# First phase of an attention-and-MLP kernel: the first two hidden pieces' products split by rows of x and put between the units, one score bank instead of two, more idle transposes, another order

## Chip, cores and metric

One core of one Trainium2 chip. The metric is device time in microseconds of one execution. Three runs of the kernel before took 499.43, 497.88 and 498.04 us (median 498.04).

## What is computed

```python
f = 1 / (1 + exp(-f_logit))                        # (4, 8, 768, 48): batch, head, time, dim
for t in range(768):
    state = f[t][:, None] * state + outer(k[t], v[t])
    y[t] = q[t] @ state
x = y.transpose(0, 2, 1, 3).reshape(3072, 384)     # 8 heads of 48
out = relu(x @ w_in) ** 2 @ w_out                  # w_in 384 x 2048, w_out 2048 x 384
```

## The kernel before

**Tiling.** Time is cut into 6 blocks of 128 steps; a block has 512 tokens (4 batches of 128). A block's attention is done in 4 units: units 0 to 2 of a block hold two heads' 48 rows on partitions 0 to 47 and 64 to 111 and, in the 16 rows behind each, a slice of two more heads; unit 3 of a block works on those slices, which DMAs gather into `last_kq`, and has no gates, keys and queries of its own. Units are numbered through: 0 to 3 are block 0, 4 to 7 block 1. In tile names `ds1_0` is block 1, unit 0 of it, that is unit 4.

**The MLP.** The hidden layer is cut into 16 pieces of 128. `up` multiplies a piece of w_in with the block's x: x has three tiles of 128 rows, and each product is three matmuls of fp32r halves (low by high, high by low, high by high), so nine matmuls of 128x512 into one bank `ph`. `square` (ACT, three passes) and `rest` (DVE) make the halves of relu squared, `down` adds nine matmuls into three banks `po`. The weights come as fp32 words in 64-bit form and are decoded on the chip by ACT and DVE (`bits`, `parts`), 12 of the 32 halves before the main passes, in five steps each.

**The first phase.** Blocks 0 and 1 of the attention, the decoding of six pieces and these pieces' products with block 0 stand in two lists of steps, `FIRST` and `SECOND`, executed by `step`; they set by hand the order on TensorE (PE), VectorE (DVE), ScalarE (ACT) and the DMA queue of SyncE (SP). GpSimd (POOL) is ordered by a scheduler. Behind `SECOND`, `flow` runs the main passes: nothing but products, with the later blocks' attention hooked in.

A step is a letter and a number, of the unit or of the piece:

- L, f, k, v load a unit's data, i and o a piece's halves of w_in and w_out (SP). G is the sigmoid (ACT). K and Q are keys and queries: a scan and a product each on DVE, and the reciprocal of Q waits for POOL.
- T transposes the keys (PE), N copies them out (ACT). S and D are the score and state matmuls (PE) into one pair of banks `ds`; M masks the scores and C updates the states (DVE).
- r and s bring rows of queries and states across the partitions: ACT copies in block 0, DMAs in block 1. m gathers a unit's slices into `last_kq`.
- Y gives the outputs (PE), H casts them to the high half of x (ACT); z takes that off on PE in block 0, and X writes the low half (ACT in block 0, DVE in block 1). g and h move unit 3's rows into x by DMA.
- A I V c J are the five steps of decoding a half of w_in (ACT, DVE, DVE, ACT, DVE), B O Z d P of w_out, e n t a w of the rows of w_in that unit 3's tile is multiplied with (`w4`).
- u is a piece's `up` with x0, x1 and x2, U of pieces 0 and 1 the three matmuls with unit 3's tile, U of later pieces the whole `up`. R is `square`, E is `rest`, W is `down`.
- busyN is N transposes of the identity that nobody reads.

In PSUM the first list has one bank `ps_h0` for `ph`, one for the key transposes, a pair that `first_py` and then all of block 1's `ds` and `py` share, and two pairs (`ps_p`, `bufs=2`) for `ds` of units 0 to 3. `ps_h1` and the three `ps_o` are opened behind `FIRST` in the place of `ps_p`. The idle transposes write into the bank of piece 0. `finish_last` copies out the last block: tile 2 in two halves by ACT and DVE, both into one tile `ob`.

Of the kernel before, what the change touches and what calls it, by code (L numbers as in the profile page):

```python
# [13 lines left out]
F32 = mybir.dt.float32  # L14
# [10 lines left out]
P = 128  # L25
# [7 lines left out]
NT = B * TB  # L33
# [3 lines left out]
NJ = DM // P  # L37
# [41 lines left out]


class Moe:
# [268 lines left out]
    def finish_last(self, c, dst):  # L350


        nc, half = self.nc, NT // 2
        self.cur = c
        for e in range(NJ):
            self.down(c.fs[-1], (e,))
        for e in range(NJ):
            ob = self.const.tile([P, NT], F32, tag=f"w{2 + e}_0", name=f"ob{c.blk}_{e}")
            if e < NJ - 1:
                (nc.vector.tensor_copy if e % 2 else nc.scalar.copy)(out=ob, in_=c.po[e])  # L360
                nc.sync.dma_start(dst(e), ob)
                continue
            nc.scalar.copy(out=ob[:, :half], in_=c.po[e][:, :half])  # L363
            nc.vector.tensor_copy(out=ob[:, half:], in_=c.po[e][:, half:])  # L364
            nc.sync.dma_start(dst(e)[:, :half], ob[:, :half])
            nc.sync.dma_start(dst(e)[:, half:], ob[:, half:])
# [10 lines left out]
def fast_path(ctx, psum, tc, moe, ident, low, flag, fkqT, vN, w, w4, out):  # L377
    nc = tc.nc
# [310 lines left out]
    half = list(range(LO)), list(range(LO, NF))  # L689
# [8 lines left out]
    def unit(n):  # L698
        if n not in units:
            units[n] = Unit(n, xs, (ps_a, ps_p) if n < HP else (ps_a,))  # L700
        return units[n]

    def step(t):

        nm = t.rstrip("0123456789")
        n = int(t[len(nm) :])
        if nm == "busy":
            if 0 not in moe.cur.ph:
                moe.bank(0)
            for _ in range(n):
                nc.tensor.transpose(out=moe.cur.ph[0][:, 0:P], in_=ident, identity=ident)
        elif nm in ("i", "o"):
            weights_load(n, "io".index(nm))  # L720
# [249 lines left out]
@with_exitstack  # L970
def tile_kernel(ctx: ExitStack, tc: tile.TileContext, fkqT, vN, w, w4, out):
    nc = tc.nc
    const = ctx.enter_context(tc.tile_pool(name="const", bufs=1))
    ident = const.tile([P, P], F32, name="ident")
    low = const.tile([P, NBLK * NJ, B * NC], F32, name="low")
    sums = const.tile([P, 2 * NF], F32, name="sums")
    flag = const.tile([1, 1], I32, name="flag")
    moe = Moe(ctx, tc, const, sums, out)
    with ExitStack() as fast:
        last, rv = fast_path(fast, ctx, tc, moe, ident, low, flag, fkqT, vN, w, w4, out)  # L980

# [6 lines left out]
    last.g[NF - 1] = moe.held  # L990
    moe.finish_last(last, lambda e: out[last.blk, e * P : (e + 1) * P])
# [61 lines left out]
```

## Time and profile before

| what | value |
|---|---|
| median of 3 runs | 498.04 us |
| profiled execution, its own time | 498.81 us |
| its span, first to last instruction | 497.1 us |
| mean granted clock of TensorE | 0.979 |
| busy: PE, DVE, ACT | 96%, 52%, 56% of the span |
| end of the step W5, first matmul of the main passes | 75.15 us |
| last matmul's end | 492.43 us |

The busy shares are means over a first phase of 75 us and a uniform rest of 417 us. The first phase has to be read by itself: by stretches, with PE's granted clock in each, and then in order of time. 1.7 us of the profiled time lie around the span.

### The profile page before, as it was taken

What the parts mean: (1) busy time and instruction counts of PE and PEld (TensorE: products, weight loads), DVE (VectorE), ACT (ScalarE), POOL (GpSimd) and SP (SyncE); (2) the same over time, 40 slices, a digit from 0 to 9 for tenths busy, and PEclk for the clock granted to TensorE, in tenths of its full rate; (3) what the DMA queues carried; (4) which work ended last, traced back from release to release, by engine and by line L of the source; (5) the groups of instructions that cost most, each with busy time, mean ns of one, the idle gap of its engine ahead of it and who ended that gap; (6) DMA issues with size and microseconds to landing.
All of it is one profiled execution on the core that took longest, in us unless ns stands there. A gap on an engine that the chain in (4) does not pass through costs nothing. (4 is left out here: it accounts for less than half of the span.)

```text
span 497.1 us, 11384 instructions
## 1 busy us (share of the span) xinstructions
PE 478.9 (96%) x4778; PEld 390.4 (79%) x4778; DVE 257.4 (52%) x472; ACT 280.2 (56%) x568; POOL 29.1 (6%) x66
## 2 busy tenths in 40 slices
PE   5879999999999999999999999999999999999995
PEld 4757786888888878888888888888888888888884
DVE  6998877999865363645353446254255331122111
ACT  4776667887847464555455554555546454544441
POOL 6221010001000000000000000000000000000000
PEclk8689999999999999999999999999999999999999
DMA  8876327473312204413005413004320001100001
GB/s 287 256 235 199 85 46 272 136 255 126 91 30 80 75 7 117 144 28 91 3 1 123 143 29 92 1 1 116 100 78 13 3 0 33 63 2 3 0 0 69
DMA packets 22684, 42.68 MB, mean 86 GB/s; under 512 B 4464, under 2 KB 8176, under 8 KB 22624
## 3 DMA queue, kind: packets, MB, share of 16 engines
q1 hardware_dynamic: 22176, 40.94, 27.0%
q0 software_dynamic: 448, 0.92, 0.8%
q8 instruction: 39, 0.64, 0.5%
q14 instruction: 21, 0.17, 0.1%
HBM read 31.69 MB, written 4.72 MB: 73 GB/s over the span
## 5 line engine op out<-in xcount | busy, mean ns | idle before, releaser
L251 PE MATMUL ph<-x,w 128*128 128x512 f32 x864 | 217.6, 397 | 1.2 <-DVE gl L268 1.2
L251 PEld LDWEIGHTS ph<-x,w 128*128 128x128 f32 x864 | 160.1, 189 | 35.8 <-DVE gl L268 2.0
L278 PE MATMUL po<-gh,w 128*128 128x512 f32 x570 | 175.6, 389 | 0.0
L268 DVE TENSOR_TENSOR gl<-ph,gh 128x512 fp32r<-128x512 f32 x95 | 65.6, 690 | 187.7 <-ACT gh L263 183.2
L261 ACT ACTIVATE ph<-ph 128x512 f32<-128x512 f32 x96 | 55.9, 582 | 144.9 <-PE ph L251 144.9
L278 PEld LDWEIGHTS po<-gh,w 128*128 128x128 f32 x570 | 107.1, 188 | 22.2
L278 PE MATMUL po<-gl,w 128*128 128x512 f32 x285 | 111.2, 390 | 0.0
L278 PEld LDWEIGHTS po<-gl,w 128*128 128x128 f32 x285 | 53.5, 188 | 11.2
L262 ACT ACTIVATE ph<-ph 128x512 f32<-128x512 f32 x96 | 55.9, 582 | 3.0
L263 ACT CAST gh<-ph 128x512 fp32r<-128x512 f32 x95 | 55.8, 587 | 3.0
L467 POOL TENSOR_SCALAR fkq<-fkq 128x8 f32<-128x8 f32 x18 | 11.9, 663 | 306.3 <-DVE fkq L462 305.8
L176 ACT CAST w<-wa 128x384 fp32r<-128x384 f32 (+1 forms) x33 | 16.6, 512 | 14.1 <-DVE wa L163 10.3
L462 DVE TENSOR_TENSOR_SCAN fkq<-fz,dr 128x520 f32<-128x520 f32 x18 | 22.2, 1235 | 4.0 <-ACT fz L457 4.0
L603 PEld LDWEIGHTS py<-sc,vn 64*64 64x64 f32 (+1 forms) x640 | 18.1, 126 | 7.1 <-issue 7.1
L476 DVE TENSOR_TENSOR_SCAN fkq<-fz,dz 128x520 f32<-128x520 f32 x18 | 22.4, 1242 | 0.6
L565 DVE TENSOR_TENSOR sc<-ds,mask 128x512 f32<-128x512 f32 x24 | 16.6, 690 | 11.1 <-PE ds L558 9.3
L603 PE MATMUL py<-sc,vn 64*64 64x64 f32 (+1 forms) x640 | 21.4, 222 | 0.0
L615 PE MATMUL py<-rx,sx 48*48 48x64 f32 (+1 forms) x320 | 20.4, 217 | 0.1
L142 ACT ACTIVATE wa<-raw 128x384 f32<-128x384 f32 (+1 forms) x33 | 18.1, 551 | 2.7 <-DMA raw<-in_w_dram 2.7
L159 DVE SCALAR_TENSOR_TENSOR wa<-raw,wa 128x384 int32<-128x384 int32 (+1 forms) x33 | 18.0, 552 | 0.7
L628 ACT CAST x<-py 112x512 fp32r<-112x512 f32 x15 | 8.8, 587 | 16.7 <-PE py L615 16.7
L615 PEld LDWEIGHTS py<-rx,sx 48*48 48x48 f32 (+1 forms) x320 | 18.0, 127 | 0.2 <-ACT sx L497 0.2
(105 smaller groups left out, 399.8 us busy)
## 6 DMA issues: line engine op xcount, KB each, us to landing
fkq<-in_fkqT_dram SPq DMA_DIRECT2D x17, 768.0 KB, 5.5
raw<-in_w_dram SPq DMA_DIRECT2D x32, 384.0 KB, 3.7
vn<-in_vN_dram SPq DMA_DIRECT2D x24, 192.0 KB, 4.8
out_dram<-ob SPq DMA_DIRECT2D x14, 256.0 KB, 2.2
x<-ys SPq DMA_DIRECT2D x30, 64.0 KB, 2.4
last_kq<-fkq SPq DMA_DIRECT2D x28, 64.5 KB, 2.4
out_dram<-part SPq DMA_DIRECT2D x3, 256.0 KB, 2.1
last_kq<-fkq POOLq DMA_DIRECT2D x8, 64.5 KB, 4.3
```

Source lines behind the costliest of these rows:

```text
L142: nc.scalar.activation(a, upper_f, AF.Abs, scale=2.0**-112, **kw)
L159: nc.vector.scalar_tensor_tensor(out=h, in0=upper, scalar=-(1 << 31), in1=h, op0=ALU.bitwise_and, op1=ALU.bitwise_or)
L251: self.nc.tensor.matmul(self.cur.ph[f], lhsT=w[:, i], rhs=x[:, j], start=first and n == 0, stop=last and n == 2)
L261: nc.scalar.activation(ph, ph, AF.Relu)
L262: nc.scalar.activation(ph, ph, AF.Square)
L263: nc.scalar.copy(out=gh, in_=ph)
L268: self.nc.vector.tensor_tensor(out=gl, in0=self.cur.ph.pop(f), in1=gh.bitcast(F32), op=ALU.subtract)
L278: self.nc.tensor.matmul(c.po[e], lhsT=l, rhs=r, start=f == c.fs[0] and i == 0, stop=f in c.ends and i == 2, skip_group_check=len(c.ends) > 1,)
L462: V.tensor_tensor_scan(out=rr[:, ::-1], data0=self.fz[:, NZ * CZ : 0 : -1], data1=dr[:, ::-1], initial=0.0, op0=ALU.mult, op1=ALU.add,)
L476: V.tensor_tensor_scan(out=pp, data0=self.fz[:, : NZ * CZ], data1=dz, initial=0.0, op0=ALU.mult, op1=ALU.add)
L603: nc.tensor.matmul(self.py[h * C : h * C + m, c, b * C : (b + 1) * C], lhsT=self.vn[rows, b, h * D : h * D + m], rhs=self.sc[rows, h, b], ...
L615: nc.tensor.matmul(self.py[h * C : h * C + m, c, b * C : (b + 1) * C], lhsT=s[rows, b * D : b * D + m], rhs=q[rows], start=False, stop=b = ...
```

## The change

It does five things.

1. `up` takes the tiles of x to multiply with. Step u becomes three: p is the three matmuls with x0, q those with x1, u those with x2. p0 stands behind X0, q0 and u0 behind X1 and X2, and p1, q1, u1 and U1 ahead of Y4.
2. `ps_h1` is open from the start, so pieces 0 and 1 have a bank each in the first list.
3. `ps_p` has `bufs=1`: units 0 to 3 share one pair of banks for `ds`.
4. The bank that this frees is `idle`, which the idle transposes write. There are 91 of them in place of 19.
5. `finish_last` gives each copy a tile of its own, so the two halves of tile 2 have separate tiles.

And the two lists stand in another order; u1, U1, R0, E0, W0's forerunners, T5, D5, S5, C5 and M5 have moved from the second list into the first.

```diff
-j0 e0 n0 f0 busy11 busy3 G0 busy2 k0 t0 K0 T0 L1 Q0 G1 v0 K1 S0 N0 D0 M0 i0 A0 I0 T1 L2 o2 L4 C0
-Q1 r0 s0 G2 K2 v1 Y0 N1 H0 z0 X0 D1 S1 B2 i3 Q2 T2 busy3 m1 C1 a0 S2 A3 w0 v2 o1 N2 r1 D2 G4 I3 i1
-M1 s1 K4 v3 A1 Y1 D3 H1 C2 s2 z1 X1 r2 m0 m2 S3 r3 o0 B0 V0 M2 L5 L6 v5 Y2 H2 Q4 r4 v4 C3 s3 G5 I1
-T4 z2 X2 M3 Y3 c0 N4 K5 G6 Q5 V1 H3 z3 X3 T5 S4 D4 o3 B3 J0 m4 r5 B1 C4 c1 s4 u0 O0 U0 M4 Y4
+j0 e0 n0 t0 f0 G0 k0 busy11 a0 busy5 L1 K0 G1 T0 N0 Q0 r0 o2 v0 K1 i0 A0 B2 busy12 S0 D0 Q1 L2 L4
+M0 I0 busy12 C0 s0 v1 i1 busy8 V0 v3 i4 T1 w0 i3 G2 K2 Q2 busy8 v2 N1 c0 r1 D1 S1 C1 m0 Y0 H0 J0
+M1 T2 N2 z0 busy12 G4 o0 X0 K4 p0 S2 D2 A3 s1 Y1 H1 C2 I3 M2 m1 z1 m2 o3 r3 D3 S3 L5 L6 v5 r2 V3
+X1 s2 Y2 c3 busy7 A1 T4 Q4 I1 C3 H2 z2 X2 G5 V1 v6 M3 K5 Q5 r4 q0 u0 s3 B0 O0 Y3 H3 N4 z3 X3 c1 o1
+busy4 J1 G6 U0 S4 R0 B3 v4 D4 p1 B1 C4 E0 q1 o4 u1 U1 Z0 M4 s4 Y4 K6 H4 X4 d0 i5 i2 T5 P0 N5 O1
+busy8 D5 S5 A2 h3 busy4 r5 C5 Z1 d1 M5
...
-J1 Z0 u1 i5 V3 o5 R0 K6 H4 X4 N5 D5 S5 E0 T6 d0 P0 i2 A2 C5 c3 U1 O1 I2 W0 R1 N6 J3 M5 h3 Z1 d1 s5
-Y5 Q6 H5 X5 V2 c2 E1 g3 U3 P1 A5 v6 o4 S6 D6 M6 i4 J2 r6 C6 m5 I5 R3 E3 A4 W1 V5 O3 I4 c5 J5 U2 R2
...
+R1 W0 J3 g3 T6 I2 Q6 s5 m4 r6 N6 Y5 H5 V2 A5 c2 X5 E1 U3 A4 R3 J2 S6 D6 o5 P1 U2 R2 M6 C6 I5 E3 W1
+V5 c5 I4 s6 Y6 V4 H6 J5 v7 m6 U5 O2 Z2 X6 m5 r7 D7 S7 E2 c4 J4 U4 B4 d2 B5 R4 P2 W2 M7 C7 O5 O3 O4
...
-    def up(self, f, last=True):
+    def up(self, f, js=range(NJ), last=True):
...
-        for j in range(NJ):
+        for j in js:
...
-            ob = self.const.tile([P, NT], F32, tag=f"w{2 + e}_0", name=f"ob{c.blk}_{e}")
...
+            for n in (slice(0, NT),) if e < NJ - 1 else (slice(0, half), slice(half, NT)):
+                ob = self.const.tile([P, n.stop - n.start], F32, tag=f"w{2 + at}_0", name=f"ob{c.blk}_{at}")
+                (nc.vector.tensor_copy if at % 2 else nc.scalar.copy)(out=ob, in_=c.po[e][:, n])
+                nc.sync.dma_start(dst(e)[:, n], ob)
+                at += 1
...
-                nc.tensor.transpose(out=moe.cur.ph[0][:, 0:P], in_=ident, identity=ident)
+                nc.tensor.transpose(out=idle, in_=ident, identity=ident)
...
-        elif nm == "u":
-            moe.up(n, last=False)
+        elif nm in "pqu":
+            moe.up(n, ("pqu".index(nm),), last=False)
...
-    moe.psum(psum, "ps_h0")
+    moe.psum(psum, "ps_h0", "ps_h1")
...
-        with tc.tile_pool(name="ps_p", bufs=2, space=bass.MemoryType.PSUM) as ps_p:
+        with tc.tile_pool(name="ps_p", bufs=1, space=bass.MemoryType.PSUM) as ps_p:
+            idle = ps_p.tile([P, 512], F32, tag="idle", name="idle")[:, :P]
...
-        moe.psum(psum, "ps_h1", "ps_o")
+        moe.psum(psum, "ps_o")
```

How it moves instructions, at three places. The first is PE around the first transposes and scores (pk is a unit's transposed keys, ds its scores and states, py or first_py its outputs). Before, from the end of D0:

```order
L547 MATMUL ds0_0_189<-vn0_0_183,kn0_0_206 64x48
L517 MATMUL pk0_1_233<-ident_58,fkq0_1_177 128x128 x4
L603 MATMUL first_py_125<-sc0_0_225,vn0_0_183 48x64 x4
L615 MATMUL first_py_125<-fkq0_0_146,sp0_73 48x64
L615 MATMUL first_py_125<-rx0_0_249,sx0_75 48x64
```

and with the change:

```order
L545 MATMUL ds0_0_221<-vn0_0_195,kn0_0_185 64x48
L714 MATMUL idle_143<-ident_58 128x128 x20
L515 MATMUL pk0_1_296<-ident_58,fkq0_1_173 128x128 x4
L714 MATMUL idle_143<-ident_58 128x128 x8
L545 MATMUL ds0_1_329<-vn0_1_279,kn0_1_322 64x48
```

Unit 1's scores now stand ahead of unit 0's outputs, and 28 idle transposes stand between the scores of units 0 and 1.

The second is PE around the products of pieces 0 and 1 (ph0_0 and ph0_1). Before, from the end of D4 to Y4:

```order
L547 MATMUL ds1_0_589<-vn1_0_524,kn1_0_567 64x48
L251 MATMUL ph0_0_148<-x0_0_116,w0_0_565 128x512 x3
L251 MATMUL ph0_0_148<-x0_1_117,w0_0_565 128x512 x3
L251 MATMUL ph0_0_148<-x0_2_118,w0_0_565 128x512 x3
L251 MATMUL ph0_0_148<-ys0_3_579,w4_343 128x512 x3
L603 MATMUL py1_0_659<-sc1_0_657,vn1_0_524 64x64
```

With the change the products of piece 0 with x0, x1 and x2, and with unit 3's tile, stand in three pieces, of which these are the last two, and D4 is followed by piece 1:

```order
L515 MATMUL pk1_0_585<-ident_58,fkq1_0_259 128x128 x4
L632 MATMUL first_py_125<-x0_2_118,minus_136 112x256 x2
L252 MATMUL ph0_0_424<-x0_1_117,w0_0_325 128x512 x3
L252 MATMUL ph0_0_424<-x0_2_118,w0_0_325 128x512 x3
L601 MATMUL first_py_125<-sc0_3_604,vn0_3_292 48x64 x4
```

```order
L632 MATMUL first_py_125<-ys0_3_651,minus_136 112x256 x2
L714 MATMUL idle_143<-ident_58 128x128 x4
L252 MATMUL ph0_0_424<-ys0_3_651,w4_166 128x512 x3
L556 MATMUL ds1_0_672<-fkq1_0_259 64x64 x16
L545 MATMUL ds1_0_672<-vn1_0_697,kn1_0_653 64x48
```

```order
L545 MATMUL ds1_0_672<-vn1_0_697,kn1_0_653 64x48
L252 MATMUL ph0_1_715<-x0_0_116,w1_0_659 128x512 x3
L252 MATMUL ph0_1_715<-x0_1_117,w1_0_659 128x512 x3
L252 MATMUL ph0_1_715<-x0_2_118,w1_0_659 128x512 x3
L252 MATMUL ph0_1_715<-ys0_3_651,w4_166 128x512 x3
L601 MATMUL py1_0_743<-sc1_0_739,vn1_0_697 64x64
```

Twelve matmuls of piece 0 have gone from behind S4 and D4 to ahead of them, and the twelve of piece 1, which stood behind Y4 in two parts, are together ahead of it.

The third is DVE from the end of Q5 to M4 (wa and w are weights in decoding, sc the masked scores, gl what `rest` writes). Before:

```order
L479 TENSOR_TENSOR fkq1_1_487<-fkq1_1_487 128x512
L159 SCALAR_TENSOR_TENSOR wa1_0_404<-raw1_0_393,wa1_0_404 128x384
L178 TENSOR_TENSOR w0_0_565<-wa0_0_229,w0_0_565 128x384
L580 TENSOR_TENSOR sp0_73<-state0_79,fkq1_0_242 112x192
L587 TENSOR_TENSOR state0_79<-sp0_73,ds1_0_589 112x192
L580 TENSOR_TENSOR sp0_73<-state0_79,fkq1_0_242 112x192
L587 TENSOR_TENSOR state0_79<-sp0_73,ds1_0_589 112x192
L152 SCALAR_TENSOR_TENSOR wa0_1_481<-wa0_1_481,raw0_1_479 128x384
L565 TENSOR_TENSOR sc1_0_657<-ds1_0_589,mask_69 128x512
```

and with the change:

```order
L477 TENSOR_TENSOR fkq1_1_538<-fkq1_1_538 128x512
L153 SCALAR_TENSOR_TENSOR wa0_1_623<-wa0_1_623,raw0_1_417 128x384
L179 TENSOR_TENSOR w1_0_659<-wa1_0_582,w1_0_659 128x384
L578 TENSOR_TENSOR sp0_73<-state0_79,fkq1_0_259 112x192
L585 TENSOR_TENSOR state0_79<-sp0_73,ds1_0_672 112x192
L578 TENSOR_TENSOR sp0_73<-state0_79,fkq1_0_259 112x192
L585 TENSOR_TENSOR state0_79<-sp0_73,ds1_0_672 112x192
L269 TENSOR_TENSOR gl0_0_690<-ph0_0_424,gh0_0_689 128x512
L160 SCALAR_TENSOR_TENSOR wa0_1_623<-raw0_1_417,wa0_1_623 128x384
L563 TENSOR_TENSOR sc1_0_739<-ds1_0_672,mask_69 128x512
```

Before, V1 and J0 stood between Q5 and C4; they have gone ahead of Q5, O0 and J1 stand in their place, and E0 with Z0 has come between C4 and M4.

## Rows read from the trace of the kernel before

**Rows 1.** From the profile's page: busy time of each engine, and the span in 40 slices of 12.4 us (busy tenths of PE, granted clock of PE in tenths).

```profile
PE 478.9 (96%) x4778; PEld 390.4 (79%) x4778; DVE 257.4 (52%) x472; ACT 280.2 (56%) x568; POOL 29.1 (6%) x66
...
PE   5879999999999999999999999999999999999995
...
PEclk8689999999999999999999999999999999999999
```

**Rows 2.** Busy time of each engine by stretch of the span: from:to, length, busy us and instructions, granted clock of PE, DMA share, GB/s.

```profile
8.50:22.06 13.56, 11.19 (x205) 9.01 (x209) 12.92 (x21) 8.86 (x23) 3.76 (x8) 0.50 0.97 330
22.06:32.32 10.26, 7.22 (x278) 5.92 (x272) 9.76 (x17) 9.12 (x22) 2.02 (x4) 1.00 0.79 241
32.32:39.10 6.78, 6.03 (x79) 5.07 (x77) 5.78 (x13) 4.00 (x10) 1.94 (x5) 0.50 0.58 146
39.10:75.20 36.10, 35.03 (x562) 27.87 (x562) 30.04 (x60) 23.99 (x52) 3.90 (x8) 1.00 0.40 112
75.20:492.50 417.30, 415.68 (x3654) 339.08 (x3652) 193.93 (x352) 230.78 (x456) 11.54 (x24) 1.00 0.22 67
```

**Rows 3.** PE in order of time, from S4 to the first matmul of the main passes: start, duration of the group, engine, line, operation, tiles, count, idle time before it and what ended that. S4, u0, U0, u1, T6, U1, the end of D6, and the first products of the main passes.

```profile
34.69 1.13 PE L558 MATMUL ds<-fkq 48*64 48x64 f32 x32
36.58 3.54 PE L251 MATMUL ph<-x,w 128*128 128x512 f32 x9
39.95 0.86 PE L251 MATMUL ph<-ys,w 112*128 112x512 f32 x3
...
41.84 2.33 PE L251 MATMUL ph<-x,w 128*128 128x512 f32 x9
...
45.19 0.66 PE L517 MATMUL pk<-ident,fkq 128*128 128x128 f32 x4
45.60 0.93 PE L251 MATMUL ph<-ys,w 112*128 112x512 f32 x3
...
54.34 0.37 PE L547 MATMUL ds<-vn,kn 64*64 64x48 f32 x10 [1.04 <-issue]
...
75.15 4.24 PE L251 MATMUL ph<-x,w 128*128 128x512 f32 x18
```

**Rows 4.** The same view of PE earlier: the first idle transposes, T0, and z2 (the matmuls that take off the high half of x2).

```profile
1.59 3.64 PE L718 MATMUL ph<-ident 128*128 128x128 f32 x16 [1.59 <-POOL ident masks.py:199]
8.37 1.07 PE L517 MATMUL pk<-ident,fkq 128*128 128x128 f32 x4 [3.14 <-DVE fkq L468]
...
28.75 0.49 PE L634 MATMUL first_py<-x,minus 112*112 112x256 f32 x2 [0.17 <-ACT x L628]
```

**Rows 5.** DVE in order of time: the end of K1, then without a gap C3, I1 (a decoding step), M3, K5 and Q5 to the step behind it.

```profile
11.62 0.69 DVE L468 TENSOR_TENSOR fkq<-fkq 128x512 f32<-128x512 f32 x1
...
28.75 0.35 DVE L580 TENSOR_TENSOR sp<-ds,last_kq 112x192 f32<-112x192 f32 x1
29.14 0.35 DVE L587 TENSOR_TENSOR state<-sp,ds 112x192 f32<-112x192 f32 x1
29.41 0.55 DVE L152 SCALAR_TENSOR_TENSOR wa<-wa,raw 128x384 int32<-128x384 int32 x1
29.88 0.68 DVE L565 TENSOR_TENSOR sc<-ds,mask 128x512 f32<-128x512 f32 x1
30.48 1.23 DVE L462 TENSOR_TENSOR_SCAN fkq<-fz,dr 128x520 f32<-128x520 f32 x1
31.74 0.69 DVE L468 TENSOR_TENSOR fkq<-fkq 128x512 f32<-128x512 f32 x1
32.56 0.21 DVE L474 RECIPROCAL dz<-fkq 128x8 f32<-128x8 f32 x1
...
34.69 0.55 DVE L159 SCALAR_TENSOR_TENSOR wa<-raw,wa 128x384 int32<-128x384 int32 x1
```

**Rows 6.** ACT in order of time: the first pass of a decoding (step B0), H2, G5, and the two copies of N4.

```profile
27.02 0.57 ACT L142 ACTIVATE wa<-raw 128x384 f32<-128x384 f32 x1
...
28.13 0.57 ACT L628 CAST x<-first_py 112x512 fp32r<-112x512 f32 x1
...
29.56 0.63 ACT L457 ACTIVATE fz<-fkq 128x512 f32<-128x512 f32 x1
...
30.97 0.53 ACT L523 COPY kn<-pk 128x448 f32<-128x448 f32 x1
31.40 0.28 ACT L525 COPY last_kn<-pk 128x128 f32<-128x128 f32 x1
```

**Rows 7.** DMA issues in short stretches, KB each and us from issue to landing: v1, issued at 6.83; v4, issued from 30.97; the second DMA of s6.

```profile
vn<-in_vN_dram SPq DMA_DIRECT2D x1, 192.0 KB, 11.2
...
vn<-in_vN_dram SPq DMA_DIRECT2D x1, 192.0 KB, 3.1
...
sx<-sp SPq DMA_DIRECT2D x1, 39.0 KB, 1.9
```

**Rows 8.** All engines in order of time at the end: the copies of the two halves of output tile 2, and the issues of their DMAs.

```profile
492.50 0.37 ACT L363 COPY ob<-po 128x256 f32<-128x256 f32 x1 [0.80 <-DVE ob L360]
492.91 0.42 DVE L364 COPY ob<-po 128x256 f32<-128x256 f32 x1 [0.40 <-ACT ob L363]
492.97 0.39 SPq L365 DMA_DIRECT2D out_dram<-ob  x1
493.45 0.41 SPq L366 DMA_DIRECT2D out_dram<-ob  x1
```

More of the change, by code (lines that the diff above doesn't have):

```diff
@@ L67 @@
 FIRST = """
-j0 e0 n0 f0 busy11 busy3 G0 busy2 k0 t0 K0 T0 L1 Q0 G1 v0 K1 S0 N0 D0 M0 i0 A0 I0 T1 L2 o2 L4 C0
-Q1 r0 s0 G2 K2 v1 Y0 N1 H0 z0 X0 D1 S1 B2 i3 Q2 T2 busy3 m1 C1 a0 S2 A3 w0 v2 o1 N2 r1 D2 G4 I3 i1
-M1 s1 K4 v3 A1 Y1 D3 H1 C2 s2 z1 X1 r2 m0 m2 S3 r3 o0 B0 V0 M2 L5 L6 v5 Y2 H2 Q4 r4 v4 C3 s3 G5 I1
-T4 z2 X2 M3 Y3 c0 N4 K5 G6 Q5 V1 H3 z3 X3 T5 S4 D4 o3 B3 J0 m4 r5 B1 C4 c1 s4 u0 O0 U0 M4 Y4
+j0 e0 n0 t0 f0 G0 k0 busy11 a0 busy5 L1 K0 G1 T0 N0 Q0 r0 o2 v0 K1 i0 A0 B2 busy12 S0 D0 Q1 L2 L4
[4 more added lines that the diff above has]
+busy8 D5 S5 A2 h3 busy4 r5 C5 Z1 d1 M5
 """
 SECOND = """
-J1 Z0 u1 i5 V3 o5 R0 K6 H4 X4 N5 D5 S5 E0 T6 d0 P0 i2 A2 C5 c3 U1 O1 I2 W0 R1 N6 J3 M5 h3 Z1 d1 s5
-Y5 Q6 H5 X5 V2 c2 E1 g3 U3 P1 A5 v6 o4 S6 D6 M6 i4 J2 r6 C6 m5 I5 R3 E3 A4 W1 V5 O3 I4 c5 J5 U2 R2
-m6 O2 V4 Z2 s6 v7 r7 Y6 H6 c4 X6 E2 J4 U5 d2 D7 S7 P2 U4 M7 C7 Z3 B4 B5 R4 s7 W2 O4 O5 d3 Z4 Z5 d4
-d5 P3 Y7 E4 H7 X7 g7 h7 P4 R5 E5 W3 W4 P5 W5
+R1 W0 J3 g3 T6 I2 Q6 s5 m4 r6 N6 Y5 H5 V2 A5 c2 X5 E1 U3 A4 R3 J2 S6 D6 o5 P1 U2 R2 M6 C6 I5 E3 W1
+V5 c5 I4 s6 Y6 V4 H6 J5 v7 m6 U5 O2 Z2 X6 m5 r7 D7 S7 E2 c4 J4 U4 B4 d2 B5 R4 P2 W2 M7 C7 O5 O3 O4
+Z3 d3 Z4 P3 d4 s7 Y7 P4 Z5 H7 X7 E4 R5 E5 W3 W4 g7 d5 P5 W5 h7
 """
@@ L356, in finish_last @@
             self.down(c.fs[-1], (e,))
+        at = 0
         for e in range(NJ):
-            ob = self.const.tile([P, NT], F32, tag=f"w{2 + e}_0", name=f"ob{c.blk}_{e}")
[L359 to L366, printed above, removed]
+            for n in (slice(0, NT),) if e < NJ - 1 else (slice(0, half), slice(half, NT)):
[3 more added lines that the diff above has]
+                at += 1
 def chunks(t):
@@ L714, in step @@
         if nm == "busy":
-            if 0 not in moe.cur.ph:
-                moe.bank(0)
             for _ in range(n):
-                nc.tensor.transpose(out=moe.cur.ph[0][:, 0:P], in_=ident, identity=ident)
+                nc.tensor.transpose(out=idle, in_=ident, identity=ident)
         elif nm in ("i", "o"):
```

## The prediction, made before the change was run

> **What bounds the kernel now.** I read the page first: PE is busy 96% of the span, and its slices are 9 from the third on [rows 1]. Then the stretches, cut where the granted clock changes: behind 39.10 PE runs at 1.00 and is busy 35.03 of 36.10 us, and behind 75.20 it is busy 415.68 of 417.30 [rows 2]. There PE is the limit at its full clock, and apart from the last output copies nothing in the change touches that part. So the change is worth what it moves the handover, the first matmul of the main passes at 75.15 [rows 3]. Ahead of 39 it is otherwise: from 8.50 to 32.32 DVE is busy 12.92 of 13.56 and 9.76 of 10.26 us, while PE stands at the half clock (0.50) up to 22.06 and again from 32.32 to 39.10 [rows 2]. DVE's chain of scans sets the pace there.
>
> Third, PE in order of time: from S4 at 34.69 to the handover PE has work without a gap, but for 1.04 us in the middle of D6 that wait for nothing the profile shows [rows 3]. So the handover is the start of S4 plus the work behind it. I forecast both.
>
> **The work behind S4.** Before it takes 75.15 - 34.69 = 40.5 us. Of that 4.4 us, up to 39.10, run at half clock, which costs 2.2; the stall costs 1.0. Left are 37.2 us of work at full clock. From there the change takes away: u0, nine matmuls, 2.3 us by u1, and U0, three, 0.8 us by the 0.93 of U1 less its latency; they now stand ahead of S4. It brings T5 behind S4, 0.7 us by T6, and 8 + 4 idle transposes. Sixteen took 3.64 us at the start, 0.23 each [rows 4]; T0 took 1.07 there and T6 takes 0.66 at full clock [rows 3, 4], so I take 0.11 each at full clock, 1.4 together. 37.2 - 3.1 + 0.7 + 1.4 = 36.2 us.
>
> **When S4 starts.** Up to the end of K1 at 12.3 [rows 5] DVE's order is unchanged. The prices of DVE's steps, start to start [rows 5]: C in block 0 0.66, a decoding step 0.47, M 0.60, K 1.9, Q 2.1, with about 0.2 when Q has to wait for POOL. Behind K1 now come Q1 (end 14.6), M0, I0, C0, V0, w0 (17.1), K2, Q2 (21.2), C1, J0, M1, K4 (24.8), C2, I3, M2, V3, Q4 (29.6), I1, C3, V1, M3 (32.3), K5, Q5 (36.8), O0, J1 (37.7), C4.
>
> Does PE deliver in time with one score bank and the idle transposes in its queue? T0 at 8.37, 12 idle ones at half clock to 12.0, S0 and D0 to 14.0 at 1 us each: M0 at 14.6 isn't held. By then PE has worked since 8.37; before it worked from 18.1 to 22.06 and the clock rose [rows 2], so I take the full clock from 14 on. 20 idle ones and T1 end at 16.9, N1 at 17.8, D1 waits for v1, which landed at 6.83 + 11.2 = 18.0 [rows 7]; it is the tenth load from the queue in both orders, with the same bytes ahead. S1 ends at 19.3, ahead of C1 at 21.2. Moving o2 ahead of v0 and L2 makes those about 1 us later, hidden: D0 wants v0 at 13. Y0, T2, z0 and 12 idle ones end at 23.0, X0 at 23.2, p0 at 23.9; S2 and D2 end at 25.1, which holds C2 by 0.3. Y1, z1, D3 and S3 end at 28.4, ahead of C3. ACT holds DVE twice: a decoding is 1.1 us there, H 0.6, G 0.6, N 0.7 [rows 6]; A1 ends at 30.0 and holds I1 by 0.4, G5, behind H2 and X2, ends at 32.6 and holds K5 by 0.3. The SP queue: v4 takes v3's buffer and waits for Y3 at 34.1, with o4 and s4 behind it; it lands 3.1 later [rows 7], 37.2, as D4 wants it. L6 waits for Y1 until 26.2, and K6 needs it at 41.
>
> S4 needs X3. M3 ends at 32.3, s3, behind G5, at 32.85; Y3 takes 1.0 (before: from the end of U0, 40.81, to u1 [rows 3]), to 34.0; then H3, N4, X3 on ACT to 36.0, U0 to 36.75. **S4 starts at 36.75**, 2.1 us later than now, since q0, u0 and more decoding stand ahead of it.
>
> **The sum.** 36.75 + 36.2 = 72.95. D5 waits about 0.3 for N5, behind Y4, H4 and d0; hand-overs take 0.2. Behind Y5 no other engine is late: W4's E4 is nearest, 0.1 ahead. Handover at 73.45: **1.7 us earlier**. The part below 39 at full clock pays 2.2 and the stall 1.0; the later S4 takes 2.1 of it, T5 and idle transposes 2.1, and u0 and U0 ahead of S4 give 3.1.
>
> **The tail.** DVE's half copy waited for ACT's, 492.91 against 492.50 [rows 8]; with tiles of its own it runs beside it. But SP issues the two DMAs one behind the other: the second at 493.45 can't go before the first ends at 493.36. Worth 0.05, at most 0.1. Extra matmuls of u cost nothing: the same nine, into the same bank.
>
> The profiled execution took 498.81, its span 497.1; less 1.75 that is 497.06. The median of the runs is 0.77 below the profiled time, so I predict **496.3**.
>
> **Bounds.** The unknown prices are the moment at which the clock rises, the stall, and the waits between engines in the new order. At best the three holds of DVE (1.0 us) and the wait at D5 vanish and X3 comes 1.0 earlier: 1.3 more, 495.0; idle transposes at nothing would be another 1.4, 493.6. At worst, below, 499.2 and more.
>
> [...] The row shows 1.04 us in the middle of D6 with nothing awaited [rows 3]. [...] 72 more transposes, each with its weight load, shift which instruction stands where.
>
> **Rivals.**
> - *Same: the gain is spent on small waits.* A stall like that of D6 comes again (1.0), or the chain to S4 is late by as much: ACT has A3, s1, H1, r3, r2, X1, s2, c3, A1, H2, X2, G5 in one line, and each late one holds DVE, which has no slack until 32 [rows 2]. For it: ACT's line has no gap of 0.3 in my working. Against it: DVE's steps are as long as before, and E0 and M4 only come at 39. Gain 0.3 to 0.9: 497.1 to 497.7.
> - *Slower: the idle transposes hold PE back because the clock doesn't rise at 14.* Between T0 and D1 stand 40 of them, 9.1 us at half clock and 4.4 at full. At half clock up to 22.06 as before, T1 ends at 19.4, N1 at 20.2, D1 and S1 at 22.2, Y0, T2, z0 and 12 idle ones at 26, S2 and D2 at 28.0: C2, I3, M2, K5 and so S4 are 2.9 later. Handover at 76.3, 1.2 later than now: 499.2. From a rise at about 23.5 on it is slower than now by over 1.5 us; at 26, with Y0, T2, z0 and 12 idle ones at half clock as well, by some 4, 502. For it: the first 16 ran at half clock for 3.64 us. Against it: PE worked as long before the rise at 22.06 as it will have at 14. [...]
> - *More: the chain to S4 is shorter*, by the bound above, 495.0.
> - *The change doesn't do what it says.* p0, q0 and u0 could stand ahead of S4 without PE being idle there, if DVE waits for S2 and D2: that is the 0.3 at C2, already in.
>
> **Chances.** The forecast with the case of more gain, over 0.3% faster (1.5 us, about what a measurement of this kernel can tell from no change): 0.48. The small waits, within 0.3%: 0.34, with the clock rising late but by 23 among it. Slower by over 0.3%: 0.18, nearly all of it the clock or a wait on PE's queue that I don't see. The range of 8 in 10 goes from 494.3, most of the better bound, to 499.6, the slower rival's 499.2 and a little: what is left out is 502 and the case without idle transposes' price. The forecast's own range is 495.0 to 497.0.
>
> **What would show it.** Right: S4 near 36.7 with PE's clock at 1.00 from about 14 and no fall to 0.50 behind it; p0 near 23.5; C1 without an idle row ahead of it; PE's rows without a gap from D5 to the first main product, near 73.5. The clock falls or rises late: 0.50 behind 20. The small waits: idle of DVE in front of I1, K5 and C2 of more than 1.0 in all, or an "issue" gap on PE. The forecast is wrong if S4 starts behind 38.2, or if PE waits for E or P steps behind Y5.

## The result: slower, and where the time went

The kernel after takes 501.44 us (median of 14 runs, 499.49 to 503.33), the one before 498.02 (14 runs, 497.31 to 502.83): ratio 1.0053, 95% interval 1.0028 to 1.0077. The forecast was 496.3 with a range to 499.6: wrong, on the side of the slower rival. The profiled execution took 502.85 us, its span is 501.1 us against 497.1; 3.41 of the 4.0 us lie ahead of the handover. The 14 times of the kernel after fall into two groups, six at 499.49 to 500.32 and eight at 501.20 to 503.33; the profile is of the upper one, and no run of the lower one has a profile.

PE's slices on the page of after, and then its stretches, cut where its granted clock changes and at the handover (columns as in [rows 1] and [rows 2]):

```profile
PE 483.6 (97%) x4850; PEld 394.9 (79%) x4850; DVE 258.2 (52%) x472; ACT 280.3 (56%) x568; POOL 29.5 (6%) x66
...
PEclk9989999999999999999999999999999999999998
...
q8 instruction: 40, 0.66, 0.5%
```

```profile
13.30:29.99 16.69, 14.09 (x392) 12.17 (x386) 15.82 (x27) 10.53 (x26) 2.96 (x6) 1.00 0.93 282
29.99:33.80 3.81, 1.30 (x21) 1.22 (x21) 2.36 (x6) 1.43 (x4) 0.54 (x1) 1.00 0.68 235
33.80:37.20 3.40, 3.40 (x13) 2.71 (x11) 0.94 (x1) 2.04 (x5) 0.00 (x0) 0.50 0.53 114
37.20:78.56 41.36, 40.09 (x694) 31.76 (x693) 35.78 (x70) 29.20 (x66) 6.36 (x13) 1.00 0.43 107
78.56:496.60 418.04, 415.89 (x3654) 338.87 (x3652) 193.88 (x352) 230.68 (x456) 11.55 (x24) 1.00 0.22 67
```

The clock is at 1.00 from 13.3 on, where it was 0.50 up to 22.06 in [rows 2], as forecast. (Ahead of 13.3 the trace has no record of it, and the page shows 9; T0's four transposes took 1.11 us at 8.12, T1's 0.60 at 15.75.) But in the second stretch PE is busy 1.30 of 3.81 us, and behind it stand 3.4 us at 0.50. PE in order of time there, p0 and the handover around it (columns as in [rows 3]):

```profile
23.42 0.96 PE L252 MATMUL ph<-x,w 128*128 128x512 f32 x3
...
32.50 0.21 PE L613 MATMUL first_py<-rx,sx 48*48 48x64 f32 x1 [2.52 <-issue]
...
33.70 0.95 PE L515 MATMUL pk<-ident,fkq 128*128 128x128 f32 x4
...
41.33 0.69 PE L556 MATMUL ds<-fkq 48*64 48x64 f32 x32
...
78.56 0.84 PE L252 MATMUL ph<-x,w 128*128 128x512 f32 x3
```

p0 starts at 23.42, as forecast, though with an unforeseen gap of 0.72 at 20.33 ahead of it. Then, in the middle of Y2, PE stands for 2.52 us and waits for nothing the profile shows, the same kind of gap as the 1.04 in D6 [rows 3]. S4 starts at 41.33, forecast 36.75. What the gap does downstream, on DVE and on ACT (columns as in [rows 5] and [rows 6]):

```profile
25.53 0.36 DVE L578 TENSOR_TENSOR sp<-ds,fkq 112x192 f32<-112x192 f32 x1 [0.39 <-PE ds L545]
...
30.86 0.56 DVE L153 SCALAR_TENSOR_TENSOR wa<-wa,raw 128x384 int32<-128x384 int32 x1 [0.85 <-ACT raw L147]
...
36.26 1.24 DVE L460 TENSOR_TENSOR_SCAN fkq<-fz,dr 128x520 f32<-128x520 f32 x1 [2.67 <-ACT fz L455]
```

```profile
33.05 0.59 ACT L626 CAST x<-first_py 112x512 fp32r<-112x512 f32 x1 [2.22 <-PE first_py L613]
35.11 0.59 ACT L640 CAST x<-first_py 112x512 fp32r<-112x512 f32 x1 [1.48 <-PE first_py L632]
35.59 0.64 ACT L455 ACTIVATE fz<-fkq 128x512 f32<-128x512 f32 x1
```

C2 is held by 0.39 (forecast 0.3), I1 by 0.85 (0.4). H2 waits 2.22 for Y2, X2 behind it 1.48, G5 stands behind both, and K5 (36.26) waits 2.67 for G5 where 0.3 was forecast.

**What the gap is.** The number of matmuls and weight loads that PE has started up to the end of each gap, from windows that begin at 0 (the counts behind the first two busy times; after up to 20.32, where a smaller gap of 0.72 ends, and up to 32.49):

```profile
0.00:20.32 20.32, 14.40 (x221) 13.26 (x221) 15.77 (x30) 9.75 (x23) 10.07 (x26) 1.00 0.91 302
0.00:32.49 32.49, 22.95 (x474) 20.30 (x475) 26.46 (x49) 17.46 (x41) 11.29 (x29) 1.00 0.88 286
```

The same of the kernel before, up to the ends of its gap of 0.30 in Y3 and of that in D6:

```profile
0.00:31.83 31.83, 21.70 (x474) 17.94 (x474) 26.70 (x49) 20.67 (x49) 11.25 (x30) 0.79 0.86 279
0.00:54.33 54.33, 42.38 (x851) 34.51 (x852) 45.77 (x84) 35.34 (x83) 16.15 (x39) 0.81 0.75 234
```

Before and after, with other steps ahead, PE stops at the same count of the two together: 948 or 949. With the waits on semaphores that the trace lists for PE, these are in front of its 449th, 961st and 1729th instruction: 512 and 768 apart, 193 + 256 k. The 256 instructions between two such counts are called a block here. And the DMA queues of after, from the moment at which PE enters the block that ends there (26.02) to 30.29, and in the microsecond behind it:

```profile
q1 hardware_dynamic: 711, 1.45, 99.6%
```

```profile
q1 hardware_dynamic: 229, 0.39, 98.7%
q8 instruction: 1, 0.02, 6.2%
```

Queue q8, of the kind "instruction", brings 16 KB packets, 40 in the span; between the first and the 38th of them the trace has 9281 matmuls and weight loads of PE, with its waits 9370: 253 to a packet. That such a packet brings PE's next block is read from these counts and from the order in time; what is in a packet, the trace does not tell. This one comes 4.28 us after PE entered the block before, in which 1.45 MB of the loads o3, L5, L6, v5 and v6 were moved; it ends at 31.32, and PE goes on at 32.50. All 18 profiles of this study show that order at this place: PE enters the block, then a packet of q8 is moved, then 1.18 us or more pass before PE goes on with the next block. Between 26.02 and 29.99 PE goes through 256 small matmuls, loads and waits in 4.0 us; before, the same number took 7.1 (24.46 to 31.55, a wait of 1.47 for X2 among it), so that a packet as late, 29.57 to 30.53, cost 0.30.

### The profile page after: what moved, and what is told of

Read it like the earlier page. It is cut to its first block, busy times and chain, and to the rows that moved or that the text cites. A ratio compares the mean times of both kernels' runs of the same rounds, so it can differ in the third digit from the quotient of the medians.

```text
span 501.1 us, 11524 instructions
## 1 busy us (share of the span) xinstructions
PE 483.6 (97%) x4850; PEld 394.9 (79%) x4850; DVE 258.2 (52%) x472; ACT 280.3 (56%) x568; POOL 29.5 (6%) x66
```

## Experiments

Theory: TensorE's next block of instructions is late because its transfer stands behind loads. Rival: something that Y2 reads is late. Edits of the lists are cut to the steps that move; all are made to the kernel after unless said.

**Six idle transposes at the start instead of sixteen**, so every block boundary falls 20 instructions later in the program; then the same kernel again for a second profile; then 22 fewer, 44 instructions.

```diff
-k0 busy11 a0 busy5 L1
+k0 busy6 a0 L1
```

```diff
-k0 busy11 a0 busy5 L1 ... i1 busy8 V0 ... Q2 busy8 v2
+k0 busy6 a0 L1 ... i1 busy2 V0 ... Q2 busy2 v2
```

> The changed kernel with 6 idle transposes ahead of T0 in place of 16: 20 PE instructions fewer (10 transposes, 10 weight loads), nothing else. PE's 2.52 us gap in the middle of Y2 stood before its 961st instruction, and in the kernel before the gaps of 0.30 and 1.04 us stood before the 961st and the 1729th (3 blocks of 256 apart). Theory, instruction blocks: PE goes on with a new block of 256 instructions there and waits for it; the gap stays at the 961st instruction, so in the program it comes 20 instructions later, still in Y2, of 2 to 3 us, and the time stays within 1.5 us of the changed kernel's. Rival, a hidden wait of Y2 on data (rows brought across, the single score bank): the gap stays at the same matmul of Y2, then the 941st instruction.

> The same kernel as the run with six idle transposes first, whose times fell into two groups, 498.6 to 499.4 and 502.3 to 503.6; the profile showed one of the lower group, with a gap of 1.08 at 29.95. If this profile is of the higher group, theory: the block of instructions lands later, the gap before the 961st instruction is over 2 us and S4 starts 1.5 us or more later, or the clock falls after it. Rival: the first phase is as before and the 4 us lie behind the handover.

> The changed kernel with 22 of the 91 idle transposes left out (10 at the start, 6 ahead of V0, 6 behind Q2), 44 instructions of TensorE with their weight loads; no DMA is moved. Theory of the blocks: every place at which TensorE can wait for a block moves 44 instructions later in the program, so that the block that came at 32.50 is wanted only at the end of Y2 or in T4, at about 31.2 to 31.7, and the gap there is under 0.8 us; the one of 0.72 at 20.33 shrinks too. S4 starts at 36.8 to 37.8, the handover comes at 73.9 to 75.0. Rival (something that Y2 reads is late): the gap stays in the middle of Y2, at the same matmul, at over 1.5 us. If the idle transposes are what holds the clock up, the granted clock rises later than 14 or falls in between, and the work up to 30 is later by more than 0.5 us.

The first took 502.62 us (10 runs), ratio 1.008 (1.005 to 1.0109), with times in two groups, 498.58 to 499.38 and 502.30 to 503.55, nothing between. Its profiled run was one of the lower, the repeat one of the higher (503.76). PE in the two profiles, the gap and the first u-products with unit 3's tile (U0):

```profile
29.95 0.21 PE L613 MATMUL first_py<-fkq,sp 48*48 48x64 f32 x1 [1.08 <-issue]
...
36.42 0.96 PE L252 MATMUL ph<-ys,w 112*128 112x512 f32 x3 [0.23 <-ACT ys L640]
37.31 0.69 PE L556 MATMUL ds<-fkq 48*64 48x64 f32 x32
```

```profile
33.37 0.26 PE L613 MATMUL first_py<-fkq,sp 48*48 48x64 f32 x1 [5.18 <-issue]
...
41.89 0.97 PE L252 MATMUL ph<-ys,w 112*128 112x512 f32 x3 [0.23 <-ACT ys L640]
```

Both gaps stand in front of the 961st instruction, 20 later in the program than in after. One kernel, one place, 1.08 and 5.18 us: U0 at 36.42 and 41.89, handover at 74.69 and 80.13. The packet came 2.79 us after PE entered the block (24.93) in one, and 6.71 us after (24.25) in the other; in those 6.71 us 2.07 MB were moved. So the size of this wait differs between executions, by 4.10 us here, of the 5.2 between the two times. That it makes the two groups is the likely reading; each group has one profile. The third run took 501.75 (498.08 to 503.01), ratio 1.0049 (1.0012 to 1.0086). Its gap stands 44 instructions later in the program, no more in Y2 but in T4, at the same count:

```profile
33.90 0.44 PE L515 MATMUL pk<-ident,fkq 128*128 128x128 f32 x2 [1.79 <-issue]
```

```profile
0.00:33.89 33.89, 21.91 (x474) 19.77 (x475) 27.21 (x50) 17.80 (x42) 12.10 (x29) 0.90 0.87 278
```

The rival falls: what T4 and Y2 read has nothing in common, the count has. The size (under 0.8 expected) was missed: D1 started as in after (17.92 for 17.99), but behind a wait of 3.60 us for v1, where after has idle transposes and 0.77; the clock was at 0.50 from 17.0 to 23.8, as expected for the case that idle transposes hold it up (one profile does not show that they do), and what followed came later (S4 at 41.24).

**L5 early and o3 late**, so that fewer bytes are queued when PE enters the block; and with G5 ahead of H2 and X2 besides.

```diff
-G4 o0 X0 K4 ... m2 o3 r3 D3 S3 L5 L6 v5 ... r4 q0 u0
+G4 o0 L5 X0 K4 ... m2 r3 D3 S3 L6 v5 ... r4 o3 q0 u0
```

```diff
-busy7 A1 T4 Q4 I1 C3 H2 z2 X2 G5 V1
+busy7 A1 G5 T4 Q4 I1 C3 H2 z2 X2 V1
```

> The changed kernel with L5 issued ahead of X0 instead of behind S3, and o3 behind r4 instead of behind m2, so that fewer bytes are queued at 25 to 30 us. Theory (TensorE waits for its next block of 256 instructions, whose transfer stands behind L5's, L6's and o3's bytes): the transfer that ends at 31.32 now ends by 30.0, the gap of 2.52 us in Y2 shrinks to under 1.3, U0 starts near 37.5 instead of 40.44, the handover comes at 73.5 to 75.5 instead of 78.56, and the time is 2 to 4 us below the changed kernel's 501.4. Rival (the transfer of the block is late by its own, whatever is queued): the gap stays at 2.3 to 2.7 and the time within 1 us of 501.4. Risk: a load that moves behind another on SP's queue holds a later step.

> The kernel with L5 early and o3 late once more. In it L6 is issued 0.8 us after TensorE enters the block before, against 0.6 in the one with six idle transposes first. Theory: mostly the block stands ahead of L6, so most runs at 498.8 to 500.4, and one in five or fewer at 501 or more. If half of the runs lie above 501, the place of L6 right behind is enough to make the block late, whatever L5 does.

> As the run with L5 early, and G5 ahead of H2 and X2 on ScalarE. Theory: K5 comes some 1.5 us earlier than in the run with L5 early alone, but S4 waits for X3, so little is won: handover within 0.6 us of that run's. If instead the chain through K5, Q5 and S5 decides, the handover is 1 us or more earlier.

The first took 499.91 us (ratio 1.0021, 1.0005 to 1.0037), the repeat 500.14 (1.0052, 1.0024 to 1.0079; five runs at 499.42 to 500.21, one at 504.44). In both profiles the gap is gone. Queue q8's packet and the rest, from PE's entry at 24.61 to 25.54 and up to 26.72 in the first; then PE:

```profile
q1 hardware_dynamic: 58, 0.10, 36.9%
...
q1 hardware_dynamic: 22, 0.04, 7.9%
q8 instruction: 1, 0.02, 6.2%
```

```profile
30.20 0.60 PE L515 MATMUL pk<-ident,fkq 128*128 128x128 f32 x4
...
36.50 0.69 PE L556 MATMUL ds<-fkq 48*64 48x64 f32 x32
...
74.28 1.07 PE L252 MATMUL ph<-x,w 128*128 128x512 f32 x4
...
491.73 0.97 PE L279 MATMUL po<-held,w 128*128 128x512 f32 x3 [0.88 <-issue]
```

0.10 MB ahead of the packet and no wait. S4 starts at 36.50, the handover comes at 74.28, 4.28 earlier than in after and 0.87 earlier than in before. The last row takes that back: a gap of 0.88 in the last nine matmuls, in front of PE's 9791st instruction, counted as above (0.61 in after, 1.08 in the repeat, none in before). With G5 earlier as well it was 502.04 (499.32, 500.27, 503.81 and 504.15), ratio 1.0064 (1.0022 to 1.0105); the profile, of the lowest run, has no gap in Y2 and the handover at 74.66, so that K5 isn't what S4 waits for. What the two upper runs lost has no profile. In all, the seven profiles of the new order with L5 and o3 in their old places have a gap at this count, of 1.08 to 5.18 us; of the seven with L5 early five have none, and two, further below, have 2.34 and 1.45.

**Other ways to move the loads or G5**, none faster than the kernel after. L6, v5 and v6 behind r4; G5 alone ahead of H2; both.

```diff
-L5 L6 v5 r2 V3 ... V1 v6 M3 K5 Q5 r4 q0
+L5 r2 V3 ... V1 M3 K5 Q5 r4 L6 v5 v6 q0
```

> The changed kernel with the loads L6, v5 and v6 moved behind r4 on SP, so that 1.2 MB of loads are not in the DMA queues when PE asks for its next instructions at about 26.0. Instruction blocks, delayed by the loads ahead of them in the queues: the fetch lands 2 to 3 us sooner, the gap in Y2 falls from 2.5 to under 0.8, K5 starts near 33.5 in place of 36.3, and the time is 2 to 3.5 us below the changed kernel's. Rival, a hidden wait on data or the new order itself: the gap stays near 2.5 and the time within 0.7 us.

> The changed kernel with G5 moved ahead of H2 and X2 on ACT, so that K5 on DVE no longer waits for Y2 by way of ACT's queue. If the gap in Y2 costs its time by that path, the gap stays (2 to 2.6 us), K5 starts near 33.5 in place of 36.3 and the time is 1.5 to 2.7 us below the changed kernel's. If PE's lateness itself (Y2, z2, Y3 and X3) sets S4, less than 1.0 is gained.

> The changed kernel with both: L6, v5 and v6 behind r4, and G5 ahead of H2 and X2. If the prediction's working was right but for the wait on instructions, S4 starts at 36 to 38 in place of 41.3, the main passes at 73 to 75 in place of 78.6, and the time is 3 to 5 us below the changed kernel's: 0 to 1.5 below the kernel before. Rival, the new order is longer by itself: the main passes start behind 76.

They took 504.69 (ratio 1.0142, 1.0114 to 1.017), 501.68 (1.0084, 1.0042 to 1.0126) and 506.81 (1.0169, 1.0136 to 1.0202). The gap in Y2 fell to 1.26, 1.53 and 1.53, U0 came at 37.23, 38.84 and 37.39, the handover at 79.41, 76.60 and 82.42. The second moves no load, and its gap is as small as the third's, so what moving these loads took off the gap is not shown. In the second K5 starts at 32.20, 4.06 earlier than in after, but S4 only 1.60 earlier, of which 0.99 are the smaller gap: S4 waits for PE's own lateness, not for K5. In the first and the third D4 paid for it, since v4 now stands behind L6, v5 and v6 on SP's queue (the row of the first; 4.64 in the third):

```profile
42.02 0.74 PE L545 MATMUL ds<-vn,kn 64*64 64x48 f32 x32 [3.20 <-DMA vn<-in_vN_dram]
```

**Toward a better version**: L5 early with six idle transposes first; that without the 12 idle ones behind S4; that with v5 and v6 ahead of L6.

```diff
-busy8 D5 S5 A2 h3 busy4 r5 C5
+D5 S5 A2 h3 r5 C5
```

```diff
-D3 S3 L6 v5 r2 ... V1 v6 M3
+D3 S3 v5 v6 L6 r2 ... V1 M3
```

> L5 early and o3 late as before, and six idle transposes at the start instead of sixteen, so that every block of 256 instructions of TensorE ends 20 instructions later in the program. Theory: no block is late at 30 (as with L5 early), and the gap of 0.88 in the last nine matmuls goes, since the block that ended before the 9,793rd instruction now ends behind the last one: handover 73.8 to 74.6, 0.9 us off the part behind it, time 498.4 to 499.6, 0.3 to 1.5 below L5 early alone (499.9). Rival: with fewer idle transposes at the start the clock rises later and S4 starts over 1 us later: 500 to 502.

> As the run before, without the 12 idle transposes that stand behind S4 (8 ahead of D5, 4 ahead of C5). They took 1.69 us in the changed kernel, 0.14 each. If they lie on the path, the handover is 1.0 to 1.7 us earlier, at 72.3 to 73.5, and the time 497 to 498.5. If TensorE waits there for N5 or C5 anyway, or the clock falls, the handover moves by less than 0.4 us.

> The kernel with L5 early, o3 late and six idle transposes first, and besides v5 and v6 (192 KB each) issued ahead of L6 (768 KB). Theory (runs differ by whether the block's transfer stands ahead of L6's bytes or behind them): L6 is issued over 1.5 us after TensorE enters the block at 25.5, the gap before the 961st instruction is under 0.5 in every run, the group of runs at 501 to 504.4 is gone: all runs within 1.5 us of each other but one in ten, median 498.0 to 499.0. Rival (the slow group has another cause): one run in four stays 2 us or more above the fastest.

The first took 499.32 (12 runs, 497.70 to 504.39), ratio 1.0035 (1.0011 to 1.0058): S4 at 36.65, handover 74.26, no gap at the end, its last matmul at 491.55 against 492.42 in before, in a run of 498.02. Three of its 12 runs lie above 501; none of those was profiled. Without the 12 idle ones it was 502.12, ratio 1.0076 (1.005 to 1.0101), handover at 75.50, in a profile of the lower of its two groups (499.10 and 499.25, the other four 501.78 to 503.38). For the 1.69 us of the idle ones PE waits for others instead, 0.9 for N5 (kn) and 0.8 for rows of states (sx); most of the 1.24 us by which the handover is later are S4, 0.29 later, and the wait for v4, 1.1 for 0.4.

```profile
PE ds L545 <- DMA vn<-in_vN_dram: 1.1, 1, 1.1
PE ds L545 <- ACT kn L521: 0.9, 1, 0.9
PE py L613 <- DMA sx<-sp: 0.8, 1, 0.8
```

(PE's waits from 36 to 75.5: us in total, times, longest.) With v5 and v6 ahead of L6 it was 499.57 (498.94 to 501.90), ratio 1.003 (1.0015 to 1.0046), four of 12 runs above 501. Its profile, of one of these, shows the gap at 1.45, the packet 3.35 us after PE's entry at 25.61, and L6 issued 1.02 after it. The expectation (under 0.5 in every run) is missed; the rival's (one run in four stays 2 us or more above the fastest) came. Missed too is the finer theory that only L6's place decides: L6 was issued later after PE's entry than in the five profiles without a gap (0.59 to 0.79), and in those 3.35 us little was moved.

```profile
q1 hardware_dynamic: 237, 0.36, 44.2%
```

**p0 back in front of q0**, on the kernel with L5 early: the split undone.

```diff
-X0 K4 p0 S2 ... o3 q0 u0
+X0 K4 S2 ... o3 p0 q0 u0
```

> L5 early and o3 late, and the three matmuls of p0 put back in front of q0 and u0, that is the split of piece 0 undone. If TensorE was idle between X0 and D3 anyway, S4 starts 0.4 to 0.8 us later (three matmuls of 128x512 at full clock) and the handover comes as much later, time 0.4 to 0.8 above L5 early alone. If p0's place between X0 and S2 held the chain to C2 and K5, S4 starts at the same time within 0.3 us.

502.18 (ratio 1.0087, 1.0063 to 1.011), U0 at 38.71. Not conclusive: the gap was back at 2.34, at the same count, since PE entered the block at 24.92 and the packet came at 29.39, 4.47 us later, with 0.77 MB moved in between.

```profile
31.70 0.32 PE L601 MATMUL first_py<-sc,vn 64*48 64x64 f32 x6 [2.34 <-issue]
```

**One pair of score banks alone**, in the kernel before.

```diff
-tc.tile_pool(name="ps_p", bufs=2,
+tc.tile_pool(name="ps_p", bufs=1,
```

> The kernel before with only the pair of score banks made single (ps_p with one buffer), the order of the steps as it was. Scores and states of a unit then wait until the unit before has read its own: D1, S1 behind C0; D2 behind C1 and D3 behind M2 and C2. In that order DVE waits for TensorE at M2 or C3 by 0.5 to 3 us. Theory: the single pair by itself is a cost that the new order has hidden: time 0.5 to 3 us above the kernel before (498.0). Rival (the banks are why the new order is late): 3 us or more above.

500.85, ratio 1.0039 (1.0023 to 1.0056): about 2 us, as expected. PE in its profile, S2 and T5:

```profile
22.07 1.16 PE L558 MATMUL ds<-fkq 48*64 48x64 f32 x32 [0.95 <-DVE sc L565]
...
36.68 1.06 PE L517 MATMUL pk<-ident,fkq 128*128 128x128 f32 x4
```

S2 waits 0.95 until DVE has read the scores before, and D3 0.57. But what the bank costs by itself isn't separated: the trace's record of the clock begins at 41.0, and four transposes take 1.06 to 1.11 us up to 36.68, where in the kernel before they took 1.05 to 1.11 at 0.50 and 0.66 at 1.00; by that estimate this execution ran at half clock where the kernel before had 1.00 (22.06 to 32.32, [rows 2]). In the kernel after no score matmul waits for DVE; S2, behind which C2 is held by 0.39, follows p0 without a gap.

**Idle transposes alone**, in the kernel before: ten in PE's wait ahead of Y3; six more ahead of z3.

```diff
-X2 M3 Y3 c0
+X2 M3 busy10 Y3 c0
```

```diff
-X2 M3 Y3 c0 N4 K5 G6 Q5 V1 H3 z3
+X2 M3 busy10 Y3 c0 N4 K5 G6 Q5 V1 H3 busy6 z3
```

> The kernel before with 10 idle transposes ahead of Y3, where TensorE waits 1.47 us for X2, 20 instructions of TensorE with their weight loads. At 0.14 each at full clock they take 1.4 us and fill that wait. By the prediction's clock term the granted clock then stays at 1.00 behind 32 and the 6.8 us at half clock are saved, of which 2.2 us behind S4: handover near 73, time 496 to 497. If the clock's fall there costs less than the sum took, or comes all the same, the handover moves by under 1 us and the time by under 0.6. The wait for the block at 31.84 grows to 0.3 to 0.7.

> As the run before, with 6 more idle transposes ahead of z3, in the wait of 0.75 us for H3. If the clock falls in the run with the first ten alone and not here, the time is 1 to 2 us lower than there; if it holds in both, the same within 0.4 us; if the 6 take longer than the wait, 0.1 to 0.5 us more.

497.92 (496.71 to 501.16), ratio 0.9999 (0.9978 to 1.0019), and 498.09, ratio 1.0 (0.9981 to 1.0018). In the first's profile the half clock lasts 3.4 us instead of 6.8 and the handover is at 73.33, 1.8 earlier, 0.8 of it from a smaller gap in D6 (0.26); the gap in Y3 is 0.76. S4 starts as before (34.62 for 34.69), and behind it 2.5 us run at half clock for 4.4: the other 1.0 us fit the 1.9 less at half clock, each of which the sum priced at a half. In the second's profile the gap in Y3 is 2.14, with the loads unmoved, the clock falls all the same, and the handover is at 74.36. In the times, whatever the clock gives is smaller than what these waits vary by (the gap in Y3 alone 0.30, 0.76 and 2.14).

## Why the prediction was wrong, step by step

**The bound, and what counts: right.** The time follows the handover (and a tail gap). Between the handover and the last matmul's end lie 417.27 us before, 418.05 after.

**The price of the stall: wrong, and the step that failed.** "The sum" paid 1.0 back for the gap in D6 and put none into the new order. No run shows that 0: the gap in D6 did go, but one of 2.52 came in Y2, ahead of S4 where the path runs through it. The row, 1.04 with nothing awaited [rows 3], stood against it; a bound from it (one more gap, of 1.0) stood only in a rival. What I did not ask is what stands 256 instructions apart in PE's program, and how fast the new order goes through them.

**When S4 starts: 41.33 for 36.75.** The working itself holds where the block is in time: with L5 early S4 starts at 36.50, with six idle ones besides at 36.65, and in all five profiles without the gap at 36.50 to 37.37. In part that is luck: with L5 early p0 starts at 22.46, 1.0 ahead of the forecast, and the next steps lose most of it again. Of the 4.83 us between after and the first of these, 2.52 are the gap; 1.33 lie between T4 and S4 (7.63 against 6.30 us), where after runs at half clock from 33.8 to 37.2, behind the gap; the other 0.98 had come before Y2, 0.31 of it by D1 (17.99 for 17.68) and the rest by p0 (23.42 for 22.46), with the gap of 0.72 at 20.33 between them.

**The clock: right on its rise, wrong on the fall.** It was at 1.00 from 13.3 (I took 14), and the slower rival, that idle transposes hold PE back at half clock, did not happen. No fall behind was forecast. In the new order the clock fell with the gaps of 2.52 and 5.18, with 1.79 (22 fewer idle ones), with 1.45 (v5 and v6 first) and with one of the two of 1.53 (G5 alone); with the other, with 1.08 and 1.26 and with 2.34 (p0 with q0) it didn't. The 2.2 us that the sum took back from the clock fit the profile with ten idle ones ahead of Y3, as said there, but the times don't show them: the 79 runs of the kernel before beside the experiments have a median of 497.7 where the mean granted clock was 0.991 or more (28 runs), 498.6 where it was 0.983 or less (41 runs), and 499.1 in the ten between.

**The work behind S4: nearly right.** 37.23 us in after, 37.78 with L5 early, forecast 36.7 with waits. The 12 idle transposes took 1.69 us, not 1.4: the rows that the prediction cites, 0.23 at half clock and 0.66 to 1.07 for T6 and T0, give 0.14 each and not the 0.11 that it took. With L5 early PE also waited 0.3 each for v4 and for s-rows.

**The tail: wrong by little.** The copies of the two halves, with tiles of their own, still run one behind the other as in [rows 8]:

```profile
495.76 0.85 PE L279 MATMUL po<-held,w 128*128 128x512 f32 x3 [0.61 <-issue]
...
496.69 0.37 ACT L362 COPY ob<-po 128x256 f32<-128x256 f32 x1 [1.56 <-PE po L279]
497.10 0.42 DVE L362 COPY ob<-po 128x256 f32<-128x256 f32 x1 [1.16 <-ACT ob L362]
```

DVE waits for ACT, with which it now shares only the tile `po` that both read; that wasn't tried apart. And 72 more transposes have brought a block's end into the last nine matmuls, for 0.61. Its count, 9791, is not 193 + 256 k; that it is a block's end is an inference from q8's packet, which ends at 494.38, 1.38 ahead of it, and from the eight profiles with as many transposes, which all have the gap at this count (0.61 to 1.34), while the ten others have none.

**The sum.** Predicted for the profiled execution were 497.06, it took 502.85: 5.1 at the handover (78.56 for 73.45), 0.6 in the tail's gap, 0.1 around it.

**What stays open.** Without the gap in Y2 the typical time is 500 (L5 early, its ten runs in two series, one of them at 504.44, median 500.1), 1.3 below after and still above before (ratios 1.0021 and 1.0052). The second of these is no lower than after's 1.0053, so what the gap costs is shown at the handover, profile by profile, and not clear of noise in the medians; six of after's 14 runs lie at 500 too. Of what L5 early lies above before, the gap at the end is 0.9 to 1.1 us in its two profiles; the rest has no profile. So the gap is the step that the forecast lacked, but not all that kept the new order from being faster. Nor is it shown why a packet waits 3.35 us while 0.36 MB are moved, or 4.47 with 0.77; on which of the 16 DMA engines it stands, the trace does not tell. No version here beats the kernel before.

## What to carry to other kernels

A gap on TensorE that waits for nothing in the profile is to be priced, not set to zero: count the instructions up to it, and if the counts lie a fixed number apart, look where the new order puts the next ones, how densely small matmuls stand ahead of them, and which loads are queued when the block before is entered. Time loads around such places: moving two loads, of 768 and 384 KB, brought the handover 4.3 us forward from one profile to the other. Where one kernel's times fall into groups, profile a run of each.

## What the runs showed of the hardware

- TensorE's gaps with nothing awaited stand in front of its 449th, 961st and 1729th instruction, 512 and 768 apart, and queue q8, of the kind "instruction", brought 40 packets of 16 KB in after, one to 253 of TensorE's traced instructions; blocks of 256 are read from these. The packet that ends in front of the 961st instruction moved only after TensorE had entered the block before: 0.61 us after at the least, 0.93 with 0.10 MB of loads moved in between, 4.28 with 1.45 MB, 6.71 with 2.07 MB, but also 3.35 with 0.36 MB. 1.18 us or more lie between the packet's end and that instruction.
- The wait of one kernel at one place was 1.08 us in one execution and 5.18 in another, of 498.58 and 503.76 us.
- 12 idle transposes of 128x128 took 1.69 us at full clock, 0.14 each; the first sixteen of before took 3.64 [rows 4]. There the trace has no record of the clock; a single one of them took 418 ns, as those at 20.7 to 21.3 did at 0.50, where three of T4's four at 1.00 took 272 to 273.
